# A Fourier mixer with a gated channel mix on one core: order of the first inverse, place of the sigmoid table load, order of the first key mixtures

## The chip, the cores and the metric

One core of a Trainium2 chip. The metric is the device time of one execution in microseconds (us); the median of several executions is quoted. The span in a profile is some 1.8 us shorter than the time of the same execution. All executions used here are fast, with one exception: an execution of the kernel before at 749 us, left out of its ratio.

Engines: PE is the matmul engine, PEld its weight loads, DVE the vector engine, ACT the scalar (activation) engine, POOL and SP issue transfers.

## The reference, cut to what matters

```python
X = np.fft.rfft(x, axis=1)                 # x: 8 batches x 3072 x 256
Yr = Xr @ w_r - Xi @ w_i + b_r             # and Yi alike; then a soft threshold
y = np.fft.irfft(Y, n=3072, axis=1)
xk = mu_k * y + (1 - mu_k) * y_prev        # y_prev: y one token earlier; xr alike with mu_r
k = np.maximum(xk @ w_k, 0.0)
out = sigmoid(xr @ w_r2) * (k * k @ w_v)
```

## The kernel before

The Fourier transforms are matmuls with small tables, each in two steps. A batch goes through `first` or `direct` (first forward step), `middle` (second step, mixing, first inverse step, `back`), a trip through DRAM that turns the layout (`Vdr`, read back as `V2`), `last` (second inverse step), and then six tiles of 512 tokens through the channel mix (`k_unit`, `r_unit`, `v_unit`). Stages of different batches run interleaved on PE.

The kernel fixes the order of instructions of every engine while it is built, with a small clock of its own. A unit of PE work may be placed once all its `needs` have a time in `done` that has passed on that clock; `run_on` books time on ACT or DVE. The engines then execute in exactly that order, at the speed that the hardware has. If a time in `done` is too early, PE comes to a unit whose data has not landed, and everything behind it waits too.

```python
def run_on(eng, ready, us):
    free[eng] = max(ready, free[eng]) + us
    return free[eng] + 0.1

def copy(ready, out, in_, act_us, dve_us):       # empties a PSUM bank pair
    eng = cheaper(ready, act_us, dve_us)         # the one that would be done first
    ...

# middle(), back step: after the last of the six stores of a batch
def fetch(k):
    for q in (2, 3, 0, 1):
        nc.sync.dma_start(out=V2[b, q], in_=Vdr[b][:, 8 * q:8 * q + 8, :])
    done["V2", b] = k + (READ_US if b == 0 else 10.5)      # READ_US = 7.0
    ...

# mix_tokens(): one tile's inputs of the channel mix, on DVE
def one(name, m, mu, c):
    def fn(k):
        nc.vector.scalar_tensor_tensor(out=m[:, c, :], in0=df[:, c, :], scalar=mu[:, c:c + 1],
                                       in1=yp[:, c, :], op0=ALU.mult, op1=ALU.add)
        ...
for i, (name, m, mu) in enumerate((("xk", xk, muk), ("xr", xr, mur))):
    for c in range(NCD):
        at(e + (2 * i + c) * 0.75, one(name, m, mu, c))    # others may come between

# r_unit(): the first sigmoid of the kernel; the tables before it were those of Sin
nc.scalar.activation(rg, ps, AF.Sigmoid, bias=0.0, scale=1.0)
```

## Time and profile before

| | before |
|---|---|
| median of 4 executions beside the change | 598.83 us (597.34 to 599.54) |
| PE busy | 572.2 of 595.5 us |
| PE idle, 40 to 55 / 55 to 59 / 59 to 62.5 / 62.5 to 75.4 / 75.4 to 80 us | 1.53 / 2.36 / 0 / 0 / 1.36 us |
| granted clock, 59 to 62.5 us | 0.51 |

PE is the bound, so what counts is PE's idle time and the clock it gets. An idle figure is the length of a stretch less PE's busy time in it. The prediction shows the lines.

### The profile page before, as it was taken

How to read it: one execution, taken by the hardware profiler on the slowest of the kernel's cores; microseconds unless marked ns; L12 is line 12 of the kernel's file. 1: busy time of each engine (PE TensorE's matmuls, PEld its weight loads, DVE VectorE, ACT ScalarE, POOL GpSimd, SP SyncE). 2: the span in 40 equal slices, each digit the busy share in tenths (PEclk: the TensorE clock that was granted, in tenths of full speed). 3: DMA queues.
4: the chain of work that ended last, by engine and by line, in shares of the span. 5: the costliest groups of instructions: out<-in, count | busy, mean ns of one | idle time of the engine just before them, and what ended most of it. 6: DMA issues, size and time to landing. Idle time of an engine off the chain costs nothing.

```text
span 595.5 us, 12379 instructions
## 1 busy us (share of the span) xinstructions
PE 572.2 (96%) x4891; PEld 431.7 (72%) x4891; DVE 520.6 (87%) x836; ACT 426.3 (72%) x467; POOL 23.4 (4%) x53
## 2 busy tenths in 40 slices
PE   4988999999999999999999999999999999999996
PEld 3877857777767787677777777677777788776665
DVE  7687989888998999988998989988999889979883
ACT  6875995767777777686777687767776867767652
POOL 7000000000000000000000000000000000000000
PEclk9999999999999999999999999999999999999999
DMA  8936869845689565983578855785348823462223
GB/s 147 167 74 156 177 129 251 168 100 114 135 188 211 134 133 124 241 204 66 120 157 239 173 111 121 164 227 133 92 94 240 173 59 72 98 169 71 67 56 91
DMA packets 68878, 84.06 MB, mean 141 GB/s; under 512 B 9042, under 2 KB 53844, under 8 KB 68820
## 3 DMA queue, kind: packets, MB, share of 16 engines
q1 hardware_dynamic: 62916, 68.98, 46.2%
q0 software_dynamic: 5712, 14.03, 14.9%
q8 instruction: 38, 0.62, 0.4%
q10 hardware_dynamic: 192, 0.26, 0.2%
q14 instruction: 20, 0.16, 0.1%
HBM read 50.07 MB, written 47.19 MB: 163 GB/s over the span
## 4 chain that ended last, share of the span: by engine, by line
PE 74%; ACT 5%; DVE 3%; issue 1%; DMA 1%; SPq 0%; ACTq 0%; DVEq 0%
PE banks L668 26%; PE banks L624 23%; PE banks L422 10%; PE banks L651 5%; ACT rl L630 3%; PE banks L279 3%; PE banks L461 3%; PE banks L394 2%; PE banks L538 2%; ACT rg L656 2%; DMA out_dram<-o 1%; DVE xk L602 1%; DVE k L636 1%; DVE xr L602 1%; DVE o L679 0%
## 5 line engine op out<-in xcount | busy, mean ns | idle before, releaser
L630 ACT ACTIVATE rl<-banks 128x1024 bf16<-128x1024 f32 x192 | 193.8, 1029 | 92.3 <-PE banks L624 84.6
L624 PE MATMUL banks<-xk,wk 128*128 128x512 bf16 x768 | 193.4, 379 | 1.6 <-DVE xk L602 0.7
L668 PE MATMUL banks<-wv,k 128*128 128x256 bf16 x1536 | 183.0, 273 | 0.6 <-ACT A L226 0.3
L668 PEld LDWEIGHTS <-k 128*128 128x128 bf16 x1536 | 149.3, 98 | 29.2 <-issue 1.2
L636 DVE TENSOR_TENSOR k<-rl 128x1024 bf16<-128x1024 bf16 x192 | 130.2, 684 | 12.0 <-ACT rl L630 11.8
L624 PEld LDWEIGHTS <-wk 128*128 128x128 bf16 x768 | 73.7, 98 | 60.0 <-issue 2.4
L422 PEld LDWEIGHTS <-XT 128*128 128x128 bf16 x768 | 74.5, 98 | 16.4 <-issue 0.7
L422 PE MATMUL banks<-wr,XT 128*128 128x256 bf16 x384 | 73.3, 272 | 0.4 <-ACT A L226 0.2
L422 PE MATMUL banks<-wi,XT 128*128 128x256 bf16 x384 | 73.3, 273 | 0.0
L602 DVE SCALAR_TENSOR_TENSOR xk<-diff,muk,YT 128x512 bf16<-128x512 bf16 x96 | 68.9, 744 | 0.2
L602 DVE SCALAR_TENSOR_TENSOR xr<-diff,mur,YT 128x512 bf16<-128x512 bf16 x96 | 68.9, 743 | 0.0
L679 DVE TENSOR_TENSOR o<-banks,rg 128x1024 f32<-128x1024 f32 (+1 forms) x49 | 58.6, 1195 | 3.6 <-PE banks L668 3.3
L226 ACT ACTIVATE YT<-banks 128x768 bf16<-128x768 f32 x59 | 45.1, 831 | 11.2 <-PE banks L538 8.3
L439 ACT ACTIVATE z<-banks 128x1024 bf16<-128x1024 f32 x35 | 35.8, 1024 | 23.4 <-PE banks L422 23.2
L651 PE MATMUL banks<-wrm,xr 128*128 128x256 bf16 x384 | 49.8, 272 | 0.3 <-ACT A L226 0.3
L656 ACT ACTIVATE rg<-banks 128x1024 bf16<-128x1024 f32 x48 | 49.2, 1024 | 0.0
L226 ACT ACTIVATE XT<-banks 128x1024 bf16<-128x1024 f32 (+2 forms) x43 | 40.6, 950 | 9.8 <-PE banks L394 9.5
L226 ACT ACTIVATE A<-banks 96x1024 bf16<-96x1024 f32 (+1 forms) x40 | 40.7, 1021 | 8.3 <-PE banks L279 6.2
L651 PEld LDWEIGHTS <-xr 128*128 128x128 bf16 x384 | 37.3, 98 | 12.1 <-issue 0.4
L226 ACT ACTIVATE V<-banks 128x1024 bf16<-128x1024 f32 x36 | 37.1, 1030 | 11.0 <-PE banks L461 10.0
L597 DVE TENSOR_TENSOR diff<-YT 128x1024 bf16<-128x1024 bf16 x48 | 32.8, 683 | 2.9 <-ACT YT L226 2.8
L451 DVE TENSOR_TENSOR Y<-z,Y 128x1024 bf16<-128x1024 bf16 x48 | 33.2, 692 | 1.7
(100 smaller groups left out, 443.8 us busy)
## 6 DMA issues: line engine op xcount, KB each, us to landing
out_dram<-o SPq DMA_DIRECT2D x188, 128.0 KB, 2.3
xs<-in_x_dram POOLq DMA_DIRECT2D x32, 384.0 KB, 6.5
Vdr<-V SPq DMA_DIRECT2D x192, 64.0 KB, 1.8
V<-Vdr SPq DMA_DIRECT2D x32, 384.0 KB, 6.7
Adr<-A SPq DMA_DIRECT2D x24, 384.0 KB, 5.4
A<-Adr SPq DMA_DIRECT2D x48, 192.0 KB, 5.2
wk<-in_moe_w_k_dram POOLq DMA_DIRECT2D x1, 512.0 KB, 12.5
wv<-in_moe_w_v_dram POOLq DMA_DIRECT2D x1, 512.0 KB, 13.7
```

Source lines behind the costliest of these rows:

```text
L226: nc.scalar.activation(out, in_, AF.Copy, bias=0.0, scale=1.0)
L422: nc.tensor.matmul(o, lhs, w[:, c, :], start=(w is wr and c == 0), stop=(w is wi and c == NCD - 1))
L439: nc.scalar.activation(z, ps, AF.Copy, bias=0.0, scale=1.0)
L451: nc.vector.tensor_tensor(out=y, in0=z, in1=y, op=ALU.subtract)
L602: nc.vector.scalar_tensor_tensor(out=m[:, c, :], in0=df[:, c, :], scalar=mu[:, c:c + 1], in1=yp[:, c, :], op0=ALU.mult, op1=ALU.add)
L624: nc.tensor.matmul(ps[:, 512 * f:512 * f + 512], wk[:, c, 128 * ff:128 * ff + 128], xk[:, c, :], start=(c == 0), stop=(c == NCD - 1))
L630: nc.scalar.activation(rl, ps, AF.Relu, bias=0.0, scale=1.0)
L636: nc.vector.tensor_tensor(out=k2, in0=rl, in1=rl, op=ALU.mult)
L651: nc.tensor.matmul(ps[:, 256 * q:256 * q + 256], xr[:, c, 128 * q:128 * q + 128], wrm[:, c, :], start=(c == 0), stop=(c == NCD - 1))
L656: nc.scalar.activation(rg, ps, AF.Sigmoid, bias=0.0, scale=1.0)
L668: nc.tensor.matmul(ps[:, 256 * q:256 * q + 256], K2[t][:, ff, 128 * q:128 * q + 128], wv[:, ff, :], start=(ff == 0), stop=(ff == NCF - 1))
L679: nc.vector.tensor_tensor(out=o[:, lo:hi], in0=ps[:, lo:hi], in1=rg[:, lo:hi], op=ALU.mult)
```

## The change: intent and diff

(a) The first inverse of batch 0 is ordered behind the landing of its reads: 10.5 instead of 7.0 on the kernel's clock. (b) A dummy sigmoid loads the table of that function early, and ACT is booked for it. A constant tile (`seli`) moves into scratch memory. This is no part of the speed: with the new `warm` tile and `seli` both kept, the kernel does not build, as memory lacks 32 bytes per partition. (c) For tile 0 alone the two halves of xk are issued together, right behind `diff`.

```diff
-    seli = const.tile([2, 2, 2, 64], FP32, name="seli")
+    seli = scs[0:2, 600:856].rearrange("p (a c r) -> p a c r", a=2, c=2)
+    warm = const.tile([128, 1], FP32, name="warm")
 ...                                                              (a)
-                    done["V2", b] = k + (READ_US if b == 0 else 10.5)
+                    done["V2", b] = k + 10.5
 ...                                                              (b)
                 if u == NU - 1:
                     done["mid", b] = end
+                    if b == 0:
+                        nc.scalar.activation(warm, n1c, AF.Sigmoid, bias=0.0, scale=0.0)
+                        run_on("act", end, 1.4)
 ...                                                              (c)
-            for i, (name, m, mu) in enumerate((("xk", xk, muk), ("xr", xr, mur))):
+            if t == 0:
+                one("xk", xk, muk, range(NCD))(e - 0.1)
+            else:
                 for c in range(NCD):
-                    at(e + (2 * i + c) * 0.75, one(name, m, mu, c))
+                    at(e + c * 0.75, one("xk", xk, muk, [c]))
+            for c in range(NCD):
+                at(e + (2 + c) * 0.75, one("xr", xr, mur, [c]))
```

More of the change, by code (lines that the diff above doesn't have):

```diff
@@ L81 @@
                    allow_small_or_imprecise_dtypes=True)
-    seli = const.tile([2, 2, 2, 64], FP32, name="seli")
+    scr = yt_pool.tile([128, 5 * N1 * 8], FP32, name="YT")
+    scs = k2_pool.tile([128, 2048], FP32, name="k2")
+    seli = scs[0:2, 600:856].rearrange("p (a c r) -> p a c r", a=2, c=2)
     nc.gpsimd.iota(seli, pattern=[[0, 2], [1, 2], [0, 64]], base=0, channel_multiplier=1,
                    allow_small_or_imprecise_dtypes=True)
-    scr = yt_pool.tile([128, 5 * N1 * 8], FP32, name="YT")
-    scs = k2_pool.tile([128, 2048], FP32, name="k2")
+    warm = const.tile([128, 1], FP32, name="warm")
     MAGIC = 12582912.0
@@ L598, in diff, with one @@
             e = run_on("dve", k, 0.69)
-            def one(name, m, mu, c):
+            def one(name, m, mu, cs):
                 def fn(k):
-                    nc.vector.scalar_tensor_tensor(out=m[:, c, :], in0=df[:, c, :], scalar=mu[:, c:c + 1],
-                                                   in1=yp[:, c, :], op0=ALU.mult, op1=ALU.add)
-                    e = run_on("dve", k, 0.745)
-                    if c == NCD - 1:
+                    for c in cs:
+                        nc.vector.scalar_tensor_tensor(out=m[:, c, :], in0=df[:, c, :], scalar=mu[:, c:c + 1],
+                                                       in1=yp[:, c, :], op0=ALU.mult, op1=ALU.add)
+                        e = run_on("dve", k, 0.745)
+                    if cs[-1] == NCD - 1:
                         done[name, t] = e
                 return fn
-            for i, (name, m, mu) in enumerate((("xk", xk, muk), ("xr", xr, mur))):
+            if t == 0:
+                one("xk", xk, muk, range(NCD))(e - 0.1)
+            else:
                 for c in range(NCD):
-                    at(e + (2 * i + c) * 0.75, one(name, m, mu, c))
+                    at(e + c * 0.75, one("xk", xk, muk, [c]))
+            for c in range(NCD):
+                at(e + (2 + c) * 0.75, one("xr", xr, mur, [c]))
         at(key, start)
```

## The prediction

> **What bounds the kernel now.** I read the page's busy shares first, then the clock row, then a table of busy time by stretch, then the waits, then the timeline of the one stretch that stood out.
>
> ```profile
> PE 572.2 (96%) x4891; PEld 431.7 (72%) x4891; DVE 520.6 (87%) x836; ACT 426.3 (72%) x467; POOL 23.4 (4%) x53
> PE   4988999999999999999999999999999999999996
> PEclk9999999999999999999999999999999999999999
> ```
>
> TensorE (PE) is busy for 572.2 of 595.5 us. So the whole span holds only 23.3 us in which PE does nothing, and no change that leaves its matmuls alone can take away more than that plus what it loses to a lowered clock. The change adds and removes no matmul. The page's slices are too coarse to show where the 23.3 us lie; the table by stretch does (columns: stretch, its length, PE, weight loads, DVE, ACT, POOL with counts, clock, DMA share, GB/s):
>
> ```profile
> 55.00:59.00 4.00, 1.64 (x22) 1.38 (x22) 1.06 (x2) 1.11 (x3) 0.83 (x3) 1.00 0.59 134
> 59.00:62.50 3.50, 3.50 (x48) 3.50 (x46) 3.43 (x12) 3.50 (x5) 1.95 (x4) 0.51 0.84 135
> 62.50:75.40 12.90, 12.90 (x108) 9.65 (x106) 12.64 (x22) 12.15 (x14) 0.00 (x0) 1.00 0.85 178
> 75.40:80.00 4.60, 3.24 (x17) 1.50 (x16) 3.67 (x7) 4.60 (x6) 0.51 (x1) 1.00 0.40 56
> ```
>
> From 80 to 590 us the same table gives PE 506.75 of 510: only 3.25 us idle. Before 55 us PE idles about 11 us, nearly all in the start-up, and after the last matmul come about 5.4 us of stores. What is left is this: 2.36 us idle in 55 to 59 (4.00 less 1.64), a stretch at half clock right behind it, and 1.36 us idle in 75.4 to 80, where ACT is busy without a gap. The change aims at just these places. The timeline of PE shows the first:
>
> ```profile
> 54.52 0.51 PE L538 MATMUL banks<-FI,V 96*128 96x96 f16 x8
> 56.02 0.34 PE L538 MATMUL banks<-FI,V 96*128 96x96 f16 x4 [0.99 <-DMA V<-Vdr]
> 57.73 0.34 PE L538 MATMUL banks<-FI,V 96*128 96x96 f16 x4 [1.37 <-DMA V<-Vdr]
> ```
>
> L538 is the last step of the inverse of batch 0. It needs four reads back from DRAM, issued from 48.90 to 50.62; the third lands at about 56.0 and the fourth at about 57.7. PE stands for 0.99 + 1.37 = 2.36 us, and matmuls of batch 1 (L422 at 57.91) stand behind it although the first half of the same unit ran at 53.65. The other place is in ACT's timeline:
>
> ```profile
> 72.67 1.02 ACT L630 ACTIVATE rl<-banks 128x1024 bf16<-128x1024 f32 x1
> 73.72 1.28 ACT L656 ACT_TABLE_LOAD   x1
> 75.01 1.02 ACT L656 ACTIVATE rg<-banks 128x1024 bf16<-128x1024 f32 x1
> ```
>
> The sigmoid table is loaded when the first sigmoid comes up, at the moment when ACT is the engine everyone waits for.
>
> **What the Trainium skill says.** "TensorE: Matmul & The Clock Gate", Part 2, Step-by-step: "The MATMULs themselves stay in program order". The trace agrees: see the wait above. So only another order helps. The same page, Part 1: the clock is cut to half after an idle window of some 3.4 us and restored after a busy one. The trace agrees: PE is busy 0.03, 0.34 and 0.27 us in the three microseconds from 55, and the granted clock is then 0.53, 0.50, 0.50 and 0.76 in the four from 59. "ScalarE: Activation LUTs", What ACT_TABLE_LOAD costs: 1283 ns, about 2.66 us with a drain. The trace has the 1283 ns exactly (1.28), but the work on both sides is only 1.32 us apart (73.69 to 75.01), so I use 1.32. The same page, Table sets: cheap functions are filler in every set, so an early load doesn't evict the copies and the Relu. The trace agrees so far: there are two loads in all, for 467 ACT instructions.
>
> **The change part by part.** The kernel fixes each engine's order by a small scheduling clock in its own code; the numbers in the diff (10.5, 1.4) feed that clock and are no measured times.
>
> (a) First inverse behind its reads. The scheduler is told that batch 0's reads land 10.5 us after issue instead of 7.0. From 48.90 that is 59.4, later than the 57.7 measured. PE should get other work for the hole: from the timeline, the second half of the mix (0.87 us), the back step of batch 1 whose input Y is ready at 55.24 (0.44), the next second step (0.44), a whole mix (16 matmuls, 1.75) and another back step (0.44), about 3.9 us in all, nearly enough for the time up to 59. Their evacuations fit, as DVE idles 2.94 and ACT 2.89 us just there. Gain: 2.36 us of idling. With PE busy there, the half clock has no cause. The 48 matmuls of L538 at 58.79 took 3.80 us; elsewhere 24 of them take 1.19, 43 ns apart, so at full clock 48 would take 0.21 + 47 x 0.043 = 2.2 us. That is 1.6 us, but ACT ran five of their evacuations end to end (3.71 us), so PE would partly wait for banks. I count 1.1 us (estimate from these two numbers).
>
> (b) Sigmoid table early. It takes 1.32 us out of ACT at 73.7. The PE waits in 75.4 to 80 are 0.40, 0.32, 0.32 and 0.32 us, all behind ACT's evacuations, 1.36 in sum. I count 1.0 back, since ACT stays nearly full there. The load and a tiny ACTIVATE (the smallest in the trace takes 0.27) come instead at about 43 to 45.5 us, 1.55 us together. ACT's gap there is 0.72 us, and the next is 1.80 at 49 to 50.7. DVE is full then (9.87 of 10 from 40 to 50) and cannot take over. So the copies of the first A2 tiles slip by up to 0.83 us, on which second steps wait. I charge 0.6.
>
> (c) Key mixtures of tile 0 back to back. On DVE a cast of 1.23 us sits between diff (ends 63.46) and xk (64.72 to 66.13). Without it xk is ready some 1.2 us sooner. PE was busy 12.90 of 12.90 in that stretch, so on the old order this is worth nothing; in the new one batch 1's middle runs out earlier and the first key matmuls must be there. I count 0 and take it as what protects (a).
>
> (d) The move of a constant tile into scratch costs nothing: the same instruction on POOL, long before its reader matters.
>
> Sum: -2.36 - 1.1 - 1.0 + 0.6 = -3.9 us. 599.0 - 3.9 = **595.1 us**, 0.65% less. Each microsecond gained by 80 us should reach the end, as PE is then 99% busy to 590.
>
> **The rivals.** First: the wait only changes its name. Batch 1's back steps move forward, and their stores share the DMA queue with the last read; or the scheduler still finds nothing to place. For it: the DMA share is already 0.96 to 1.10 in 51 to 56. Against: the margin of 1.7 us between 57.7 and 59.4, and that Y and the bank are free at 55.3. The time would be some 598. Second: the gain is handed back between 63 and 80, where DVE (12.64 of 12.90) and ACT (12.15 of 12.90) are as full as PE, so that PE reaches their backlog sooner and waits there. For it: ACT is never idle from 70 to 83. Against: both had almost 3 us of idle time at 55 to 58, which the new order fills with this very work, and the table load leaves. If half is lost: 597. Third: the early table load sits in front of the copy that releases batch 1's transposes (43.22) and stops PE for the full 1.3 us: then 596 to 597. Fourth: the new order spreads through the whole program, since every later choice of the scheduler follows from the earlier ones; idle time in 80 to 590 is 3.25 us now and may become 1 or 6. This is the main spread, in both directions.
>
> **Range and chances.** If all goes fully, 2.36 + 1.6 + 1.36 = 5.3 us are gained: 593.7; a better order later might give one more. If two rivals hold, nothing much is left. The three runs of before spread over 2.2 us. So 592.4 to 598.2 for 8 in 10. A gain of 2% is 12 us, more than these stretches hold (23.3 us of PE idling in all, some 16 in start-up and tail, untouched); a loss of 2% would need a new wait in every batch. Faster 0.02, within 2% 0.965, slower 0.015.
>
> **What would show it.** Right: no wait of L538 for the read at 54 to 60; granted clock 1.00 from 55 to 65; PE above 3.5 of 4 us in 55 to 59; the table load near 44 us and a sigmoid directly behind its predecessor later; PE idling under 0.5 us in the stretch that now is 75.4 to 80; the first key matmul a few us before 65.9; PE's count over the batches unchanged. Wrong: PE waits for Y or XT in place of the reads (first rival); ACT or DVE full and PE under 95% at 65 to 80 (second); PE idling over 1 us more at 43 to 48 (third); more than 5 us idle in the steady part (fourth).

## The result, and the profile after

594.96 us median of 4 executions (594.61 to 595.20) against 598.83; the ratio is 0.9938, 95% interval 0.9918 to 0.9958. Ratios here are the mean time of one kernel's fast executions over that of the other's of the same rounds, so not quite the ratio of the medians quoted. A later set of six executions beside eleven of before gave 594.67 against 598.57 us and the ratio 0.9937 (0.9924 to 0.9950).

Line numbers have moved: L538 is now L543, L624 is L635, L656 is L667. This is the table of busy time by stretch of the changed kernel (columns as in the prediction):

```profile
40.00:55.00 15.00, 12.97 (x163) 10.97 (x160) 13.48 (x18) 11.93 (x14) 0.00 (x0) 1.00 0.59 154
55.00:59.00 4.00, 3.93 (x55) 3.57 (x53) 3.79 (x6) 2.76 (x5) 2.16 (x5) 1.00 0.66 116
59.00:62.50 3.50, 2.74 (x46) 2.37 (x46) 3.43 (x11) 3.50 (x6) 0.74 (x2) 1.00 0.94 184
62.50:75.40 12.90, 12.15 (x86) 8.19 (x86) 12.57 (x22) 12.56 (x15) 0.51 (x1) 1.00 0.86 171
75.40:80.00 4.60, 4.28 (x30) 2.82 (x29) 4.60 (x7) 3.57 (x5) 0.51 (x1) 1.00 0.98 207
```

The hole at 55 to 59 is filled (3.93 of 4) and the clock stays at 1.00. But 0.76 us of idling have appeared at 59 to 62.5 and 0.75 at 62.5 to 75.4, where there was none. The timeline says what the first of these is:

```profile
56.49 0.18 POOL L490 CAST n1c<-V 96x1 f32<-96x1 bf16 x1 [41.38 <-DMA V<-Vdr]
57.75 1.19 PE L543 MATMUL banks<-FI,V 96*128 96x96 f16 x24
59.15 1.20 PE L543 MATMUL banks<-FI,V 96*128 96x96 f16 x24 [0.22 <-ACT YT L227]
60.55 0.50 PE L543 MATMUL banks<-FI,V 96*128 96x96 f16 x8 [0.20 <-ACT YT L227]
61.26 0.50 PE L543 MATMUL banks<-FI,V 96*128 96x96 f16 x8 [0.20 <-ACT YT L227]
```

The POOL cast waits for one of the four reads and so marks a landing: 56.49, over a microsecond before PE comes to the inverse at 57.75. All eight units then run in a row, and PE waits for ACT to empty banks. And ACT at the new and at the old place of the load:

```profile
43.16 1.28 ACT L499 ACT_TABLE_LOAD   x1
44.46 0.20 ACT L499 ACTIVATE warm<-n1c 128x1 f32<-128x1 f32 x1
44.56 1.92 ACT L227 ACTIVATE A<-banks 128x1024 bf16<-128x1024 f32 x2
...
71.39 1.03 ACT L641 ACTIVATE rl<-banks 128x1024 bf16<-128x1024 f32 x1
72.29 1.04 ACT L667 ACTIVATE rg<-banks 128x1024 bf16<-128x1024 f32 x1
```

The first sigmoid now follows its predecessor without a gap. At 40 to 55, PE idles 2.03 us (15.00 less 12.97) instead of 1.53.

This profile misses 67 of PE's 4891 matmul records, most of them after 80 us, so its busy sum (566.7) is not compared with that of before. The second profile of the changed kernel, used below, misses none.

### The profile page after: what moved, and what is told of

The parts are those of the page before. It is cut to its first block, busy times and chain, and to the rows that moved or that the text cites. A ratio compares the mean times of both kernels' runs of the same rounds, so it can differ in the third digit from the quotient of the medians.

```text
span 593.3 us, 12315 instructions
## 1 busy us (share of the span) xinstructions
PE 566.7 (96%) x4824; PEld 428.9 (72%) x4891; DVE 519.3 (88%) x834; ACT 425.5 (72%) x467; POOL 23.5 (4%) x53
## 4 chain that ended last, share of the span: by engine, by line
PE 81%; ACT 7%; DVE 4%; DMA 3%; issue 2%; SPq 1%; POOL 0%; POOLq 0%; DVEq 0%; ACTq 0%
PE banks L679 27%; PE banks L635 23%; PE banks L423 14%; PE banks L662 5%; PE banks L462 3%; PE banks L280 3%; PE banks L395 3%; ACT rl L641 2%; PE banks L543 2%; ACT rg L667 1%; DMA xs<-in_x_dram 1%; DMA Adr<-A 1%; ACT YT L227 1%; PE banks L353 1%; SPq L305 1%
## 5 line engine op out<-in xcount | busy, mean ns | idle before, releaser
L635 PE MATMUL banks<-xk,wk 128*128 128x512 bf16 x701 | 188.7, 379 | 5.3 <-DVE xk L608 0.7
L635 PEld LDWEIGHTS <-wk 128*128 128x128 bf16 x768 | 73.9, 98 | 60.7 <-issue 3.1
L227 ACT ACTIVATE XT<-banks 128x1024 bf16<-128x1024 f32 (+2 forms) x45 | 42.8, 956 | 9.2 <-PE banks L395 8.4
L667 ACT ACTIVATE rg<-banks 128x1024 bf16<-128x1024 f32 x48 | 49.1, 1024 | 0.0
L440 ACT ACTIVATE z<-banks 128x1024 bf16<-128x1024 f32 x32 | 32.7, 1022 | 19.9 <-PE banks L423 19.8
L227 ACT ACTIVATE V<-banks 128x1024 bf16<-128x1024 f32 x35 | 35.9, 1024 | 11.6 <-PE banks L462 10.6
```

Source lines behind the costliest of these rows:

```text
L227: nc.scalar.activation(out, in_, AF.Copy, bias=0.0, scale=1.0)
L635: nc.tensor.matmul(ps[:, 512 * f:512 * f + 512], wk[:, c, 128 * ff:128 * ff + 128], xk[:, c, :], start=(c == 0), stop=(c == NCD - 1))
```

## The experiments

Each experiment is told with PE's idle time by stretch, in one table, because the times alone are coarse (an interval of 0.2 to 0.3% is 1.2 to 1.8 us). "Half clock" says whether the clock was cut between 55 and 63 us.

| kernel | 40 to 55 | 55 to 59 | 59 to 62.5 | 62.5 to 75.4 | 75.4 to 80 | half clock | ratio to before (95%) |
|---|---|---|---|---|---|---|---|
| before, profile of record | 1.53 | 2.36 | 0 | 0 | 1.36 | yes | 1 |
| before again (e8) | 1.54 | 2.68 | 0 | 0 | 1.19 | yes | 1.0025 (1.0001 to 1.0050) |
| (a) (e1) | 1.54 | 0.22 | 0.61 | 3.42 | 0.32 | no | 0.9999 (0.9972 to 1.0026) |
| (b) (e2) | 2.03 | 0.82 | 0.41 | 0.09 | 0.32 | no | 0.9956 (0.9936 to 0.9976) |
| (c) (e3) | 2.37 | 1.53 | 0 | 0 | 1.03 | yes | 1.0022 (1.0000 to 1.0045) |
| (a) + (b) (e5) | 2.03 | 0.06 | 0.77 | 2.58 | 0 | no | 0.9974 (0.9957 to 0.9991) |
| (a) + (c) (e6) | 1.53 | 0.22 | 0.61 | 1.74 | 0.64 | no | 0.9965 (0.9946 to 0.9984) |
| (b) + (c) (e7) | 2.12 | 2.23 | 0.40 | 0.10 | 0 | no | 0.9963 (0.9940 to 0.9987) |
| all (e9) | 2.02 | 0 | 0.83 | 0.64 | 0.32 | no | 0.9937 (0.9924 to 0.9950) |
| the booking of (b) only (e12) | 2.29 | 1.66 | 0.49 | 0.60 | 0.95 | no | 0.9956 (0.9925 to 0.9986) |

The ratios come from the four sets of rounds (e1 to e4, e5 to e8, e9 to e11, e12), so two ratios of different sets were also measured on different chips. At half clock PE is busy longer with the same work, so an idle time of 0 there does not say that nothing waited.

**(a) alone.** Edit to before: only the line of (a).

> Part (a) alone: the scheduler is told 10.5 us for batch 0's reads. My theory: the wait of 2.36 us and the half clock behind it (1.1 us) go, so 3.0 to 3.5 us less than before (ratio 0.994 to 0.995), and the table load stays at some 73 us with about 1 us of PE waits behind it. Rival (the gain is handed back to ACT and DVE between 63 and 80): 1 to 2 us less. Rival (only the shuffled later order counts): no particular number, and idle time in 80 to 590 us differs from before by more than 1.5 us.

598.27 us median of 6, ratio 0.9999. My theory failed here, and the rival held more strongly than it had been put. The wait for the reads and the half clock did go, but the time did not. In the table by stretch of this run:

```profile
55.00:59.00 4.00, 3.78 (x61) 3.50 (x59) 3.90 (x6) 3.24 (x4) 1.59 (x4) 1.00 0.80 166
62.50:75.40 12.90, 9.48 (x68) 6.42 (x66) 12.17 (x19) 8.99 (x10) 0.00 (x0) 1.00 0.69 146
```

PE is busy 3.78 of 4 where it had stood, and idles 3.42 us where it had never stopped. DVE's timeline, and then PE's, give the cause:

```profile
62.89 0.75 DVE L602 SCALAR_TENSOR_TENSOR xk<-diff,muk,YT 128x512 bf16<-128x512 bf16 x1
64.27 1.23 DVE L434 TENSOR_TENSOR z<-banks,bias 128x1024 bf16<-128x1024 f32 x1 [0.62 <-PE banks L422]
65.53 0.43 DVE L450 TENSOR_SCALAR Y<-z 128x1024 bf16<-128x1024 bf16 x1
65.99 0.69 DVE L451 TENSOR_TENSOR Y<-z,Y 128x1024 bf16<-128x1024 bf16 x1
66.60 0.75 DVE L602 SCALAR_TENSOR_TENSOR xk<-diff,muk,YT 128x512 bf16<-128x512 bf16 x1
```
```profile
64.44 0.38 PE L624 MATMUL banks<-xk,wk 128*128 128x512 bf16 x1
...
67.40 2.53 PE L624 MATMUL banks<-xk,wk 128*128 128x512 bf16 x11 [2.59 <-DVE xk L602]
```

PE runs the first key matmul on the first half of xk and stands for the second half. Between the halves, DVE's fixed order has three operations of batch 1, and the first of those even waits 0.62 us for a matmul. In the kernel before, PE still had other work at that time; (a) had moved that work forward. The record of the single executions adds one thing: the two of (a) with a mean granted clock of 0.998, the profiled one among them, took 596.4 and 596.7 us, and the four with 0.992 to 0.996 took 598.0 to 601.3. This points to a cut of the clock in these four too, at a place that no profile shows.

**(b) alone.** Edit to before: the dummy sigmoid with its booking, and the moved constant tile.

> Part (b) alone, with the constant tile moved to make room: my theory says about 0.4 us less (1.0 gained at 75 to 80, 0.6 lost at 43 to 48), ratio 0.999 to 1.000; the wait for the reads and the half clock stay. Rival (the early load stops PE for its whole 1.3 us): 0 to 0.5 us more than before. Rival (the late load was worth its full PE idle time): 1.3 us less.

595.92 us median of 6, ratio 0.9956. None of the three expectations fits: the gain is 2.6 us (0.44% of 598.6), not 0 to 1.3. The local terms are as predicted: PE idles 0.5 us more at 40 to 55 (2.03 against 1.53), and 0.95 less at 62.5 to 80 (0.41 against 1.36). The rest is at the reads. They were issued at 48.23, and PE came to the inverse at 54.77, so 6.54 us after the issue instead of 5.62; and in this execution the fourth landed earlier. Only 0.73 us of the wait was left, with no half clock:

```profile
54.77 0.83 PE L543 MATMUL banks<-FI,V 96*128 96x96 f16 x12
56.33 0.34 PE L543 MATMUL banks<-FI,V 96*128 96x96 f16 x4 [0.73 <-DMA V<-Vdr]
```

So the slip that I had charged as a cost is absorbed by a wait that is there anyway.

**(c) alone.** Edit to before: only the part of (c).

> Part (c) alone: my theory says 0 within 0.3 us, as PE was busy without a gap where the first key mixtures ran. Rival (an earlier first key matmul lets the token work start sooner and matters by itself): 0.7 to 1.2 us less.

600.61 us median of 6, ratio 1.0022. No gain, as the theory said; the rival fell. The profiled execution (601.48 us) was an unlucky one, with the clock low longer, from before 59 us on, and once more near 257 us:

```profile
55.00:59.00 4.00, 2.47 (x18) 1.81 (x19) 1.48 (x5) 0.23 (x1) 1.65 (x4) 0.65 0.51 95
59.00:62.50 3.50, 3.50 (x46) 3.50 (x45) 2.44 (x9) 3.15 (x5) 1.05 (x3) 0.50 0.93 171
...
255.00:260.00 5.00, 3.46 (x34) 2.74 (x35) 2.48 (x9) 2.32 (x4) 0.00 (x0) 0.76 0.68 232
```

Up to 58 us this kernel is the one before, so this shows how much the stretch differs between executions. Part (c) doesn't explain it.

**The clock by itself.** Extra matmuls on constant tables fill the two waits; their results are overwritten by the real ones.

```diff
                 for i in range(4):
                     n2 = 16 * half + 4 * i + qd
+                    if b == 0 and n == 1 and i in (0, 2):
+                        for _ in range(22 if i == 0 else 30):
+                            nc.tensor.matmul(pv[:, 0, :, i, :], ident[:96, :], FI, start=True, stop=True)
```

> Before, with 22 and 30 extra small matmuls (results overwritten) put into the two waits for the reads, 0.95 and 1.3 us at full clock; the order and the waits stay. It parts the clock from the wait. My theory: the half clock at 59 to 62.5 goes (granted clock 1.00) and 1.0 to 1.6 us of time with it, the 2.4 us of waiting stay. Rival (in that stretch PE waits for the evacuations anyway, so the clock is worth nothing): within 0.3 us of before.

597.07 us median, but four executions are near 597.0 (granted clock 0.998 and 0.999) and two near 602 (0.995), so the ratio is 1.0006 (0.9971 to 1.0041): inconclusive by time. The profile is of one near 597, and the half clock is gone:

```profile
56.18 1.44 PE L539 MATMUL banks<-FI,ident 96*128 96x96 f16 x30
58.50 1.78 PE L541 MATMUL banks<-FI,V 96*128 96x96 f16 x32
60.47 0.86 PE L541 MATMUL banks<-FI,V 96*128 96x96 f16 x16 [0.20 <-ACT YT L226]
```

The 48 matmuls that took 3.80 us at half clock end 2.83 us after their start (61.33 less 58.50), 0.97 less. The first key matmul starts 16.61 us after the issue of the reads, against 17.04 and 17.12 in two profiles of before: 0.4 to 0.5 less. Between the two lies the waiting for ACT's evacuations. So the half clock near 59 us is worth 0.4 to 1.0 us in these profiles of the kernel before. I had counted 1.1.

**(a) + (b), without (c).** Edit to the changed kernel: (c) undone.

> Parts (a) and (b) without (c). Theory now: with (a) alone the gain came back as one wait of 2.59 us of the first key matmuls for the second half of xk, since three DVE operations of batch 1 stood between the halves; (c) is what closes that hole. So without (c) a wait of 2 to 3 us of the key matmuls for xk shows at some 65 us, and the ratio to before is 0.997 to 1.000. Rival ((c) is worth nothing in combination either): ratio as the full change, 0.993 to 0.995, and no such wait.

596.70 us, ratio 0.9974. As expected, the hole between the two halves of xk is there, again of 2.58 us:

```profile
65.03 0.38 PE L629 MATMUL banks<-xk,wk 128*128 128x512 bf16 x1
68.00 2.32 PE L629 MATMUL banks<-xk,wk 128*128 128x512 bf16 x10 [2.58 <-DVE xk L607]
```

With (c) the interval of the ratio is 0.9924 to 0.9950 (another set, another chip), without it 0.9957 to 0.9991; the two do not overlap. A part that is worth nothing alone is worth about 0.37% (0.9974 less 0.9937, some 2.2 us) on top of the other two.

**(a) + (c), without (b).** Edit to the changed kernel: the dummy sigmoid and its booking undone.

> Parts (a) and (c) without (b). Theory: no wait for xk over 0.7 us and little or no wait for the reads, half clock gone; the late table load leaves PE waits of 0.8 to 1.4 us near 73 to 80. Ratio 0.995 to 0.997. Rival ((b) carries the whole effect, as it did alone): ratio 0.998 to 1.001.

596.28 us, ratio 0.9965. As expected: no wait for the reads, none for xk over 0.7 us, and PE waits 1.7 us once for the ACT queue that holds the table load and the first sigmoid:

```profile
PE banks L631 <- ACT rg L663: 1.7, 1, 1.7
```

The idle time at 62.5 to 80 is 2.38 us, against 0.96 with (b): (b) gives back 1.4 us there, for its 0.5 us at 40 to 55. By time (b) adds 0.28% here; the intervals overlap a little (0.9946 to 0.9984 and 0.9924 to 0.9950).

**(b) + (c), without (a).** Edit to the changed kernel: 10.5 put back to READ_US for batch 0.

> Parts (b) and (c) without (a). Theory: the first inverse keeps its place ahead of the landing, the early table load only pushes PE's arrival there back by some 0.6 us, so a wait for the reads of 0.7 to 2 us is left, now and then with the half clock; ratio 0.995 to 0.998 with a spread of runs of over 2 us. Rival ((a) isn't needed when (b) is there): ratio as the full change with a spread under 1 us.

596.60 us, ratio 0.9963, with executions from 593.25 to 598.28. The expected spread is there. The waits for the reads are 0.76 and 1.57 us:

```profile
PE banks L543 <- DMA V<-Vdr: 2.3, 2, 1.6
```

No half clock followed them near 59 us (one came at 254.65 us, after waits for batch 3's reads), though in the kernel before waits of the same sum were followed by it each time. The clock entries of the fourteen traces show most of what decides this. Within one execution the clock changes only at moments that lie a whole number of 3.413 us apart, as if time were cut into stretches of that length, and where the cuts lie differs between executions. These are the stretch ahead of the half clock in before, and the two in this run that share the waits:

```profile
55.65:59.06 3.41, 1.67 (x23) 1.44 (x24) 0.88 (x2) 0.52 (x2) 0.89 (x3) 1.00 0.51 113
```
```profile
53.27:56.68 3.41, 1.98 (x28) 1.60 (x25) 1.76 (x3) 2.64 (x3) 0.00 (x0) 1.00 0.77 197
56.68:60.09 3.41, 2.43 (x41) 2.23 (x42) 2.07 (x9) 1.26 (x2) 2.05 (x5) 1.00 0.41 60
```

In before one stretch holds most of the waiting; here a cut at 56.68 divides it. Over all traces, from the first rise of the clock to 585 us, there are six stretches in which PE was busy for less than 1.7 of the 3.41 us. Five of them (1.23 to 1.67 us busy) were followed by a stretch at half clock. Of the stretches at full clock in which PE was busy for 1.98 us or more, none was. The exception is the hole of (a) alone, from 63.28 us, with 1.53 us busy and no half clock after it; why is open. So whether a wait of some 2.4 us is followed by the half clock also depends on where the cuts fall, and that is chance.

**Before again.**

> The kernel before once more, unchanged, for its profile and its spread. Theory: its profile of record (597.3 us) was one of its luckier executions; others show a longer wait for the reads (3 to 5 us in sum) and a longer stretch at half clock. Rival: the same wait of 2.4 us each time, and the spread has its cause in the start-up or in the steady part. Ratio 0.998 to 1.002.

600.00 us median of 6 (597.69 to 601.83), ratio 1.0025. The profiled execution (598.63 us) waits 2.68 us for the reads, 1.14 and 1.54, and has the half clock:

```profile
55.00:59.00 4.00, 1.32 (x17) 1.02 (x16) 0.74 (x2) 1.15 (x2) 0.45 (x2) 1.00 0.64 156
59.00:62.50 3.50, 3.50 (x44) 3.43 (x43) 3.29 (x11) 2.83 (x4) 2.32 (x5) 0.51 0.75 112
```

So neither theory nor rival as I put them: the wait is about the same, not 3 to 5 us, and this execution also waits 1.3 us for batch 3's reads near 256 us, which the profile of record did not. The profile of record (597.3 us) was a little luckier than the median. A kernel against itself gives 1.0025 here, with an interval that just misses 1; differences of 0.2% between two kernels deserve no explanation.

**The changed kernel again.**

> The changed kernel once more, beside before on one chip with five rounds, for a second profile and a firmer ratio. Theory: ratio 0.993 to 0.996, no wait for the reads at 54 to 60 us and granted clock 1.00 there, PE idle 1.5 to 2.5 us between 55 and 80 us; runs spread under 2 us, less than before's 2.5 to 5. Rival (the four runs of record were lucky and the three parts add to no more than two of them): 0.996 to 0.998.

594.67 us median of 6 (593.66 to 595.47), ratio 0.9937. All as the theory said, but for the reads of later batches: it waits for those 1.9 us in three places, most near 250 us.

**Later for the other batches too.** The same number is too early there as well, so I tried larger ones in the changed kernel.

```diff
-                    done["V2", b] = k + 10.5
+                    done["V2", b] = k + (10.5 if b == 0 else 12.5)
```

> The changed kernel with the scheduler told 12.5 us in place of 10.5 for the reads of batches 1 to 7 as well. Several profiles show the same disease once more at 250 us: the last inverse step of batch 3 reaches PE some 7 us after its reads' issue and waits 0.9 to 2.8 us for them, at times with a half clock behind it. Theory: that wait goes, 1.0 to 2.0 us less than the changed kernel (ratio to before 0.990 to 0.993). Rival (the new order of everything after batch 1 opens waits elsewhere, as with part (a) alone): within 1 us of the changed kernel or slower.

> The same with 14.5 us. Theory: as with 12.5, if the wait at 250 us is all that counts; a larger value should only help until PE runs out of other work, which would show as key matmuls or gates waiting for xk or xr at the change from one batch to the next, and a time 0 to 3 us above that with 12.5.

With 12.5: 598.41 us, ratio 1.0001, so 3.7 us slower than the changed kernel. With 14.5: 596.61 us, ratio 0.9969. In both, PE's wait for these reads is gone, and both are slower; the rival held. That 14.5 would be 0 to 3 us above 12.5 failed as well: it is 1.8 us below. Part of it is new waits for banks. This is PE's largest wait after 80 us in sum, first with 12.5, then with 14.5:

```profile
PE banks L635 <- ACT A L227: 1.1, 4, 0.3
```
```profile
PE banks L635 <- ACT YT L227: 1.3, 6, 0.2
```

But counted from 80 us to PE's last matmul, or to 590 us where that came later, 12.5 idles only about 1 us more than the changed kernel (5.51 against 4.56). The rest of the 3.7 us is inside what the profile counts as busy, and I could not place it. None of the versions tried beats the changed kernel.

**The booking of (b) without the load.** Edit to before: only `if b == 0: run_on("act", end, 1.4)`. No dummy sigmoid.

> Before with only the scheduler's entry of part (b): ACT is booked for 1.4 us behind the last inverse of batch 0, but nothing is loaded there; the sigmoid table still comes late. All engines keep the order of the run with (b) alone, bar the load. It asks why (b) alone was worth 2.6 us where I had counted 0.4. Theory (the load itself counts, by leaving 72 to 75 us and by pushing PE's arrival at the first inverse back by 0.6 us): here PE arrives early again, waits 2 us or more for the reads, mostly with half clock, and idles over 1 us near 72 to 80; ratio 0.999 to 1.002. Rival (the other order of copies counts): ratio 0.995 to 0.997.

596.94 us median, ratio 0.9956 (0.9925 to 0.9986), the same as with the load. My theory failed and the rival held: the booking alone, which only makes the scheduler hand out the copies in another order, is worth as much as (b) alone, within some 1.8 us. The local worth of the load shows in the trace: here PE idles 1.55 us at 62.5 to 80, against 0.41 with the load. Where the booking gains its time is not shown: the profiled execution (597.92 us, the slowest of the six; 67 matmul records are missing here too) idles 5.99 us at 40 to 80, against 5.25 and 5.41 in the two profiles of before. It has no half clock either, though it waits 0.47 and 1.45 us for the reads:

```profile
55.22 0.34 PE L540 MATMUL banks<-FI,V 96*128 96x96 f16 x4 [0.47 <-DMA V<-Vdr]
57.01 0.34 PE L540 MATMUL banks<-FI,V 96*128 96x96 f16 x4 [1.45 <-DMA V<-Vdr]
```

With the order of (b), three profiles of three (e2, e7, e12) have no half clock here; with the order of before, three of three have it (before, e8, e3). That fits a gain of (b) beyond its local terms, but six profiles don't prove it: here too a cut divides the waits (PE is busy 2.60 and 2.24 us in the two stretches of 3.41 us), and two of the six executions have a granted clock of 0.995 and 0.996.

## Why the prediction was right or wrong

The sum was right: 595.1 predicted, 594.96 and 594.67 measured. Several of its terms were not, and errors cancelled, so the close agreement is in part luck.

**The wait for the reads (2.36 us in step (a)).** It vanished as described. But its worth was put to (a) as if it needed nothing else, and (a) alone did not change the time (0.9999). The prediction named this as its second rival, the gain handed back between 63 and 80, and gave it half the gain; alone it took all: the idle time between 55 and 80 is 3.72 us in before and 4.57 with (a), so the loss of the half clock is about paid for by more idling. It came as one wait for the second half of xk, not as a general fullness of DVE and ACT. Even in the full change 0.76 to 0.83 us return at 59 to 62.5, since eight units in a row outrun their evacuations; the prediction had considered evacuations only for the clock.

**The half clock (1.1 us).** It vanished. Measured by filling the waits it is 0.4 to 1.0 us in the two profiles of before. Two steps were too high: the 48 matmuls were to save 1.6 us and saved 0.97, and about half of that is then waited for banks. The prediction also put the half clock to an idle window; in the stretch ahead of it PE was busy for 1.67 of 3.41 us.

**The table load (-1.0 + 0.6 in step (b)).** Both local terms are well sized: -0.95 alone or -1.4 with (a) and (c), and +0.5. What failed is the sum for (b) alone (-0.4 expected, -2.6 measured). The 0.6 us of slip is no cost as long as PE would wait for the reads at the end of it. And the booking changes the order of the copies; that alone brought the ratio of 0.9956. This is the fourth rival, order. It was expected to act through the steady part; where it acted is not shown.

**The key mixtures (0, "what protects (a)").** Right as a mechanism: 0 alone, and the hole of 2.6 us closes when it joins (a). But a term that another one needs isn't 0 in a sum; without it the full change would have given 0.26%, not 0.63%.

**The signs to look for.** Right: no wait for the read, clock 1.00, PE 3.93 of 4, the load near 44 us, the sigmoid right behind its predecessor. Partly wrong: 0.32 us idle at 75.4 to 80, but another 0.64 to 0.75 just before it. Wrong: the first key matmul did not come "a few us" earlier. It starts at 65.02 instead of 65.94, and 16.94 us after the reads' issue instead of 17.04; what changed is how much of batch 1 was done by then.

**What stays open.** From the second profiles: idle time of 40 to 80 us is 5.41 us in before and 3.81 in after, 1.60 less; with 0.4 to 1.0 for the clock that makes 2.0 to 2.6 us. These two profiled executions differ by 3.2 us (598.63 and 595.47). The remaining 0.6 to 1.2 us can be put to the start-up, where the clock is low at first and comes up at a different moment in each execution: by the traces' clock entries at 21.5 us in both profiles of before, at 18.4 and 19.0 in those of after, but also at 18.9 in (a) alone and 18.6 in (c) alone, which are the kernel before up to there. In the profiles of record, 31 transposes took 3.49 us in before and 3.14 in after:

```profile
15.85 3.49 PE L352 MATMUL banks<-ident,YT 128*128 128x128 f16 x31 [0.44 <-ACT YT L226]
```
```profile
15.79 3.14 PE L353 MATMUL banks<-ident,YT 128*128 128x128 f16 x31 [0.42 <-ACT YT L227]
```

When batch 0's reads are issued, the changed kernel is 0.82 us ahead in these two profiles and 1.08 us in the second ones. Of the three parts only (b) acts before that, and it adds idle time there, so I put this lead down to chance.

The medians differ by 3.7 to 3.9 us, and what they hold beyond 2.0 to 2.6 I can't place. The clock in other executions is one candidate: its mean is 0.9951 over the 50 fast executions of before in the four sets (those of e8 among them), and 0.9987 over the ten of after. But the 16 of before with 0.997 or more still take 598.4 us on average, against 594.7 for after, so the clock is not most of it.

By time alone, the full change (0.9924 to 0.9950) cannot be told from (b) alone (0.9936 to 0.9976) or from its booking alone (0.9925 to 0.9986). PE's idle time at 40 to 80 us doesn't part them either: 3.81 us with all, 3.67 in the profile of (b) alone, which is of its fastest execution. So it is not shown that (a) and (c) together add to (b); what the pairs show is that (c) is needed once (a) is there. All executions of the full change lie within 1.8 us in e9, those of (b) alone within 3.9.

## What to carry to other kernels

When you remove a wait of the bounding engine by reordering, ask what work fills the hole and from where it is taken: the engine will be short of it later, and the next input must be ready by then. Parts of such a change don't add; test them in pairs and read PE's idle time stretch by stretch, as the times alone cannot separate a wait that is gone from one that has moved. And in a kernel whose order comes from a cost model, each number in the model is an edit of the whole program: two "safer" numbers for later batches removed their waits and still lost 2 to 4 us.

## What the Trainium skill lacked or had wrong

- "ScalarE: Activation LUTs", What ACT_TABLE_LOAD costs: the load takes 1.28 us as stated, but the total of about 2.66 us with a drain doesn't show. Work on both sides is 1.32 us apart in before, and in the changed kernel the dummy ACTIVATE starts at 44.46, 0.02 us after the load's end.
- "TensorE: Matmul & The Clock Gate", HAM oscillation: it gives idle gaps above some 3.4 us as what to avoid. Here the clock was halved for 3.41 us (59.06 to 62.47) after gaps of only 0.99 and 1.37 us with little work between them, and not after 0.76 and 1.57 us in another order. No page says how much work holds the clock up. In these traces it was halved after five of the six stretches of 3.41 us in which PE was busy for less than 1.7 us, and after none at full clock in which PE was busy for 1.98 us or more.
- No page has it: the granted clock in the profile reads 1.00 in the first 20 us, where matmuls of 128 columns ran 110 ns apart (31 in 3.49 us, less the 0.2 of the first), against 57 ns later (16 in 1.06, likewise). The first clock entry of that trace is at 21.51 us; before it the column shows 1.00 and does not hold.
